# k^T v of two half batches in one TensorE block, with three t and kvz buffers

## The chip, the cores and the metric

The kernel runs on one core of a Trainium2 chip. The core has a matrix engine (TensorE, PE in the profile; the loads of its stationary operands are the row PEld), a vector engine (VectorE, DVE), a scalar engine (ScalarE, ACT), GpSimd (POOL) and a sync engine (SP). Each works through its own list of instructions in order, and semaphores hold an instruction back until what it needs is there. PE writes its results to PSUM, from which DVE and ACT read them. DMAs move data between device memory and SBUF; they are issued from the queues of SP and POOL. The metric is the time of one execution on the device, in microseconds (us); less is better.

## The reference

Inputs are q, k and v of 8 batches, 8 heads, 576 positions and a head size of 64, and the weights of 8 experts. First comes linear attention, then a layer of experts whose shares are balanced by eight rounds of row and column normalization.

```python
phi = lambda x: np.where(x > 0, x, np.exp(x) - 1.0) + 1.0
q_p, k_p = phi(q), phi(k)
kv = np.einsum('bhsd,bhse->bhde', k_p, v)
z = np.sum(k_p, axis=2)
num = np.einsum('bhsd,bhde->bhse', q_p, kv)
den = np.einsum('bhsd,bhd->bhs', q_p, z)[..., None] + 1e-06
x = (num / den)                      # transposed to 4608 tokens x 512
P = np.exp(x @ w_gate - max)
for _ in range(8):
    P /= P.sum(1, keepdims=True) + 1e-09
    P /= P.sum(0, keepdims=True) + 1e-09
    P *= N / E
for e in range(E):
    out += P[:, e:e + 1] * (np.maximum(x @ w1[e], 0.0) @ w2[e])
```

## The kernel before, in words

**Two parts.** The attention front produces x, transposed, in SBUF (`xT`: 128 partitions x 4 x 4608 tokens). Expert 0 is computed beside it, on the tokens that are ready, and experts 1 to 7 follow. Experts work on groups of 512 tokens: layer 1 (`hq`, L712 for the first two groups, L736 for the next, L858 for the later ones, which use a seven-product scheme for 2x2 blocks with sums prepared by DVE), then layer 2 (`ye`, L980 and L1098).

**The front** runs over 16 units (b, g): batch b and one half g of its eight heads, that is four heads. For each unit:

- k (576 KB, as f32), q and v (converted to 16 bits on the way) are loaded by DMAs issued on POOL (L386), a few of the first unit on SP. The k tiles have three buffers, q three, v three.
- ACT makes exp(k) (`ek`, L401), DVE makes max(k+1, 1) (`t`, L405) and the minimum of both (L409), which is phi(k). `t` has two buffers.
- PE forms k^T v and k^T 1 in one block (`f_kv`, L430): 18 matmuls with 64 rows each, two at a time on the upper and the lower half of the array, into a PSUM tile `kv_ps` that lies over two banks. The moving operand is the v tile, whose three planes are v, a plane of ones, and v of the other two heads. So the block is in another arrangement of the array than its neighbours, which use all 128 rows.
- Two copies (`f_z`, L337 on ACT or L339 on DVE) bring the result to SBUF as `kvz`, which has two buffers and zeros off its diagonal blocks, cleared once by DVE at the start.
- phi(q) is made likewise (L474, L477, L480), transposed by nine matmuls on PE (L485) into the two banks `att`, and copied to `qpT`.
- PE forms the denominators from `qpT` and `kvz` (`att`, L456); ACT takes Ln (L508) and Exp of the negative (L512), which is the reciprocal `rden`.
- PE forms the numerators (`num_ps`, L456), and DVE multiplies them by `rden` into `xT` (L527).

For the first two batches q, denominators and numerators are worked in two pieces, so that expert 0 can begin sooner; later ones in one or two equal halves. `kv_ps` and `num_ps` share one PSUM pool of one buffer (`p_kv`), so a numerator waits until the kvz copies are done, and a kv block until DVE has read the last numerator. After the third batch and after every odd batch PE forms the router's logits (L544).

**At the start** 40 matmuls on a tile of zeros (`yw <- warm`, L619) stand between the first instructions; their results aren't used. `warm` is 128 x 512. DVE clears the tiles and sets the three planes of ones (L631).

**The order.** Nothing is scheduled by hand in the code: `_Plan` records tasks with their engine, an estimate of their cost, what they depend on, the pools they take from and a priority, and `run` issues them in one order. For the front this order is written out, in the string `_FRONT`: each word is a task's number and its engine (p PE, a ACT, d DVE, g POOL, s SP, m a DMA in flight, n none). What comes after the front is ordered by the plan's estimates and priorities. A pool of n buffers makes a task wait for the users of the tile n places back.

**Gates.** For the last two units a tiny DMA on SP reads a corner of each loaded tile (L417), so that SP's stores behind it come after those loads; one POOL instruction (L421) does the same for POOL. Behind the gates SP stores x and its prepared sums to device memory (L759, L760, L791) for the experts 1 to 7. DVE makes these sums (L774 to L779) during and after the front.

**The end of the front.** When all of it is done its pools are closed, and two matmuls on zeros (L681) take the banks that expert 0 uses from then on.

Of the kernel before, what the change touches and what calls it, by code (L numbers as in the profile page):

```python
# [11 lines left out]
FP16 = mybir.dt.float16  # L12
# [5 lines left out]
class _Plan:  # L18
# [121 lines left out]
    1n 118n 123n 621n 44s 45m 0g 42s 43m 2p 48g 49m 3p 4p 46g 47m 5p 80g 81m 6p 7p 78g 79m 8p 57n 58a 59d 9p 82g 83m  # L140
    60d 10p 84g 85m 11p 12p 50a 51d 13p 14p 15p 16p 17p 18p 52d 19p 20p 53n 54p 63a 64d 21p 55d 22p 93n 61p 65d 128g
    129m 56a 23p 94a 62d 24p 25p 130g 131m 66p 26p 67d 86a 132g 133m 87d 68p 27p 134g 135m 28p 95d 69a 29p 88d 30p
    119g 120m 99a 71p 96d 89n 100d 90p 72a 101d 70a 164g 165m 97p 91d 102p 98d 31p 92a 166g 167m 32p 73a 103d 74p
    143n 170g 171m 104p 136a 75d 33p 34p 137d 121g 122m 76p 35p 105a 36p 77d 37p 144a 38p 107p 138d 106a 110p 168g
    169m 39p 108a 40p 111d 41p 139n 149a 145d 140p 146d 147p 141a 200g 201m 622p 148d 142a 150d 109a 124g 125m 151d
    112p 623a 152p 113d 202g 203m 624p 172a 179n 173d 204g 205m 632p 153a 174d 180a 154p 228g 229m 181d 175n 176p
    155a 182d 625d 633a 183p 177d 630p 184d 178a 156a 190p 631d 160p 232g 233m 191a 634p 161d 192a 230g 231m 157p
    635d 185a 196p 626p 258g 259m 186d 158a 187d 636p 126g 127m 197d 627a 207d 188p 637a 654n 661p 189d 159a 193p
    162p 260g 261m 628p 163d 638p 213n 206a 194a 208d 262g 263m 195a 629d 198p 640p 662a 199d 214a 114g 115m 209n
    655p 215d 216d 210p 656a 286g 287m 235d 217p 211a 657p 218d 288g 289m 663p 241n 234a 212a 236d 658d 219p 316g  # L150
    317m 237n 238p 220a 243d 664d 242a 221p 290g 291m 239d 659p 222a 244d 667p 660a 265d 223a 245p 240d 669p 116g
    117m 246d 224p 247p 225d 639p 271n 264a 248a 318g 319m 668d 226p 646a 641p 266d 272a 344g 345m 273d 249p 267n
    642p 227d 320g 321m 670a 274d 250a 268p 346g 347m 648d 275p 269a 270a 644p 299n 276d 251a 252p 277p 645p 253d
    278a 293d 292a 643p 301d 279p 687n 254p 294d 372g 373m 280a 665p 255d 300a 295n 256p 666d 322a 302d 296p 323d
    329n 257a 652a 688p 324d 400g 401m 297a 303p 298a 650d 348g 349m 281a 282p 690p 304d 376g 377m 330a 331d 675p
    357n 374g 375m 283d 691a 305p 351d 402g 403m 284p 306a 676p 285d 325n 350a 307p 332d 326p 683d 308a 430g 431m
    359d 673p 327a 689a 328d 309a 352d 333p 310p 334d 674p 378a 311d 335p 671p 379d 336a 312p 358a 337p 313d 353n
    672p 338a 360d 432g 433m 354p 339a 404g 405m 385n 361p 407d 486g 487m 355a 692p 413n 362d 356a 434g 435m 681a
    694p 387d 386a 693d 363p 380d 342p 364a 696p 460g 461m 343d 695a 314p 388d 406a 415d 340p 677p 315a 341d 381n
    414a 389p 697d 436a 495s 488g 489m 382p 390d 458g 459m 416d 365p 383a 698p 437d 366a 462g 463m 443n 384a 678p  # L160
    408d 367a 579d 391p 370p 392a 700p 371d 699a 393p 685d 496s 368p 394a 702p 369d 409n 701a 706p 438d 720n 395a
    580d 410p 586d 703a 445d 679a 417p 521g 522m 587d 411a 581d 707p 471n 412a 418d 517g 518m 444a 398p 419p 399d
    721p 420a 519g 520m 446d 472a 396p 421p 397d 439n 704p 422a 465d 440p 423a 473d 474d 447p 490g 491m 441a 722d
    705p 529g 442a 448d 464a 424p 723p 425d 534n 449p 466d 426p 450a 725p 427d 467n 714a 451p 726d 468p 452a 497s
    524d 526s 453a 475p 712d 527s 710p 528s 502n 476d 469a 582s 583m 470a 711p 724d 503a 493d 456p 477p 504d 708p
    478a 457d 535a 727p 588d 505d 589s 590m 479p 584s 585m 729p 536d 480a 537d 454p 481a 709p 591s 592m 455d 428p
    728d 492a 484p 716a 731p 485d 429a 730a 538p 494d 732a 482p 718a 539d 733p 498n 523a 483d 506p 499p 507a 525d
    600d 530n 735p 500a 501a 601d 741p 734d 761n 602d 508p 736d 603s 604m 531p 509a 605s 606m 593d 510p 532a 594d
    762p 511a 533d 595d 742p 757d 512a 596s 597m 598s 599m 515p 540p 749a 516d 764p 541a 758d 513p 765a 542p 514d
    737p 543a 759d 743p 544a 763d 547p 607d 766p 548d 744p 767a 760d 545p 608d 751a 768p 546d 770p 577n 769a 800d  # L170
    738p 609d 771a 801d 610s 611m 753d 549p 612s 613m 802d 754d 772p 550a 745a 803s 804m 551n 552d 774p 805s 806m
    773a 739p 775a 578p 755d 776p 858d 740p 756d 777a 614g 615n 618n 619g 620m 778d 808p 807n 553p 810p 809a 779d
    782p 811a 780d 822p 554d 783a 781d 816p 747a 812p 555d 788p 813a 823a 814p 786p 815a 828p 817d 556p 818p 829a
    557d 784p 789a 859d 819d 832p 785a 558d 820p 824p 792p 825a 821a 790p 860d 830p 833d 861s 862m 616g 617m 559p
    826p 1031s 1032m 793d 866p 827a 1088s 1089m 834p 560d 863s 864m 787d 867a 794p 835a 831d 870p 795a 865n 836d 880p
    871a 840p 837d 881a 561d 882p 841a 872p 883a 886p 846p 887a 884p 847a 838d 868p 873a 890p 791d 869a 850p 891d
    885a 842p 916d 917d 876p 843a 918d 892p 877d 874p 893a 888p 851d 878p 875d 852p 879a 839d 924p 889d 844p 925a
    974d 930p 894d 845a 938p 975d 853a 562p 848p 976d 931a 895d 977s 978m 928p 979s 980m 849d 923n 898p 929a 563d
    896d 939a 900p 919s 920m 899a 897d 921s 922m 944p 564d 926p 904p 927a 942p 905a 932p 901a 934p 933d 940p 908p
    935d 941a 1023d 945a 565p 936p 909d 948p 937a 902p 949d 943a 566d 982p 903a 567d 946p 983a 910p 906p 950p 981n  # L180
    947d 986p 951a 988p 911a 952d 568p 996p 987a 998p 953d 956p 997a 569d 999a 907d 984p 957a 570d 1004p 985a 962p
    989a 1002p 958p 1003a 963a 1000p 954d 959a 992p 1005d 1006p 955d 966p 1007d 964p 967d 571p 993d 960p 1024d 994p
    1025d 990p 995a 968p 1026d 1001a 991d 1008p 1033n 1034p 965d 1009a 1022n 1544n 1036p 572d 1035a 1012p 573d 1037a
    1040p 1042p 1041a 1038p 1044p 1039a 1013p 969a 1045d 574p 1043d 1010p 961d 1046p 1027d 1048p 1047a 575d 1050p
    1049a 576d 1011p 1051a 1054p 856d 1056p 1019d 1055a 1052p 651d 686a 1058p 1028d 1016p 1018a 1029d 713a 1091p
    1059d 1053a 1014p 653d 1057d 1015p 647d 1017p 854d 1020a 1092a 1093p 1021d 1090n 1547n 1060p 1094a 1030d 1097p
    1145s 1146m 1061a 1099p 1095p 1062d 1066p 1063d 1068p 1064d 1067a 1098a 1065d 1071p 649a 1101p 717a 1069d 1076p
    1070d 1096a 1102d 715a 1079p 1078d 1072a 1077d 970a 1103p 1073g 748d 1105p 750d 1107p 1548g 1549m 1100d 1106a
    1082p 1108a 682d 1104a 1111p 1084d 1113p 1081d 1112a 1109p 1080d 1074a 1115p 1083d 1110a 1075g 1148p 1114d 746a
    1150p 1116d 1085p 1149a 1151a 1117p 1087d 1147n 1154p 1086d 1118a 1202s 1203m 1156p 857a 1119d 1152p 1123p 1155a  # L190
    1120d 972d 1125p 1124a 1121d 915a 1128p 1122d 680a 1127d 1158p 1129a 684d 1133p 1153a 1126d 1130g 1159d 1136p
    1545g 1546m 1135d 1134d 1160p 1138d 1162p 1157d 1164p 1163a 1139p 752d 1165a 796d 1161a 1168p 1141d 1170p 1140d
    1169a 1166p 1131a 1172p 1167a 1205p 1173d 1207p 1206a 1137d 1142p 1208a 1174p 1143d 1204n 1211p 1171d 1175a 1259s
    1260m 1213p 913a 1144d 1209p 1176d 1180p 1212a 1177d 1182p 1181a 1178d 719a 1185p 1179d 798a 1183d 1215p 1188a
    1184d 1190p 1210a 1216d 1186a 1214d 1193p 914a 1187g 971d 1217p 1191d 1132g 1219p 1192d 1221p 1189g 1220a 1196p
    1222a 1218a 1225p 1198d 1227p 1194d 1226a 1223p 1197d 1229p 797d 1224a 1262p 1228d 1264p 1263a 1230d 1199p 1265a
    1195d 1231p 1200d 1261n 1268p 1201d 1232a 1316s 1317m 1270p 973a 1233d 1266p 1237p 1269a 1234d 1239p 1235d 1238a
# [23 lines left out]
def kernel(  # L221
# [10 lines left out]
    nc = tc.nc  # L232
# [127 lines left out]
    def att(b, g):  # L360
# [73 lines left out]
        def f_za(_):  # L434
            gz["tile"] = kvz_t[(len(p_kvz["order"]) - 1) % 2]
# [821 lines left out]
```

## Time and profile before

| what | us |
| --- | --- |
| median of three runs | 958.1 (957.68 to 958.19) |
| profiled execution, its own time | 958.06 |
| span of the profiled execution | 955.9 |
| PE busy | 947.0 |
| DVE busy | 784.1 |
| ACT busy | 583.5 |

The span runs from the first to the last instruction that the profile shows. The tables name an engine, a line of the kernel, the tile that is written and those read, how often, the busy time and the mean duration. Matmuls are pipelined: one of 512 columns is shown as 379 ns long, while the next begins 216 ns after it. So the starts of instructions tell more of PE than its busy time does.

### The profile page before, as it was taken

How to read it: one execution, taken by the hardware profiler on the slowest of the kernel's cores; microseconds unless marked ns; L12 is line 12 of the kernel's file. 1: busy time of each engine (PE TensorE's matmuls, PEld its weight loads, DVE VectorE, ACT ScalarE, POOL GpSimd, SP SyncE). 2: the span in 40 equal slices, each digit the busy share in tenths (PEclk: the TensorE clock that was granted, in tenths of full speed). 3: DMA queues.
4: the chain of work that ended last, by engine and by line, in shares of the span. 5: the costliest groups of instructions: out<-in, count | busy, mean ns of one | idle time of the engine just before them, and what ended most of it. 6: DMA issues, size and time to landing. Idle time of an engine off the chain costs nothing.

```text
span 955.9 us, 21249 instructions
## 1 busy us (share of the span) xinstructions
PE 947.0 (99%) x8634; PEld 810.4 (85%) x8634; DVE 784.1 (82%) x1508; ACT 583.5 (61%) x1047; POOL 146.8 (15%) x211
## 2 busy tenths in 40 slices
PE   8999999999999999999999999999999999999998
PEld 4765588788888888888888888888888888888886
DVE  7899999998888888878887888878887888877775
ACT  7999766576555555555555555555555555555552
POOL 7432000011102111211112111110112111111110
PEclk9999999999999999999999999999999999999999
DMA  9998492172127222542227222362226222235554
GB/s 239 265 230 179 167 251 79 39 159 68 66 75 162 76 79 78 131 113 79 79 77 167 79 78 78 95 149 77 79 78 132 95 69 73 72 99 166 166 166 110
DMA packets 47101, 112.81 MB, mean 118 GB/s; under 512 B 4444, under 2 KB 27484, under 8 KB 47004
## 3 DMA queue, kind: packets, MB, share of 16 engines
q1 hardware_dynamic: 21340, 75.84, 24.1%
q0 software_dynamic: 25264, 35.11, 19.5%
q8 instruction: 67, 1.10, 0.5%
q10 hardware_dynamic: 400, 0.52, 0.2%
q14 instruction: 30, 0.25, 0.1%
HBM read 119.69 MB, written 17.69 MB: 144 GB/s over the span
## 4 chain that ended last, share of the span: by engine, by line
PE 95%; DVE 2%; DMA 1%; ACT 1%; POOL 0%; issue 0%; SPq 0%; DVEq 0%; ACTq 0%
PE ye L1098 36%; PE hq L858 24%; PE R L858 12%; PE Zye L858 6%; PE Zye L1098 6%; PE ye L980 4%; PE hq L736 2%; PE hq L712 1%; DMA w<-in_moe_w_dram 1%; PE kv_ps L430 1%; PE att L456 1%; PE num_ps L456 1%; PE att L485 1%; DMA kin<-in_k_dram 0%; DVE xT L527 0%
## 5 line engine op out<-in xcount | busy, mean ns | idle before, releaser
L1129 DVE SCALAR_TENSOR_TENSOR acc<-ye,P_sb,acc 128x256 f32<-128x256 f32 x620 | 267.7, 479 | 123.2 <-PE ye L1098 121.8
L858 PEld LDWEIGHTS <-W 128*128 128x128 f16 x2144 | 209.8, 98 | 24.9
L1098 PEld LDWEIGHTS <-S 128*128 128x128 f16 x1984 | 194.1, 98 | 22.5
L1139 POOL TENSOR_TENSOR acc<-acc,st 128x256 f32<-128x256 f32 x124 | 88.5, 733 | 686.5 <-ACT st L1136 686.5
L1098 PE MATMUL ye<-T,S 128*128 128x256 f16 x1488 | 192.8, 273 | 0.0
L858 PEld LDWEIGHTS <-w 128*128 128x128 f16 x1608 | 157.3, 98 | 19.6 <-issue 0.5
L1098 PEld LDWEIGHTS <-h 128*128 128x128 f16 x1584 | 155.0, 98 | 18.1 <-issue 0.2
L893 ACT ACTIVATE h<-hq 128x512 f16<-128x512 f32 x134 | 80.1, 598 | 141.9 <-PE hq L858 139.2
L858 PE MATMUL R<-xs,W 128*128 128x256 f16 x1008 | 151.2, 273 | 0.0
L858 PE MATMUL hq<-xs,W 128*128 128x256 f16 x1008 | 151.2, 273 | 0.0
L858 PE MATMUL hq<-xs,w 128*128 128x256 f16 x1008 | 140.9, 273 | 0.3 <-DVE h L896 0.3
L890 ACT ACTIVATE h<-Zye 128x512 f16<-128x512 f32 x134 | 80.1, 598 | 40.0 <-PE Zye L858 40.0
L1136 ACT ACTIVATE st<-Zye,P_sb 128x256 f32<-128x256 f32 x124 | 52.6, 471 | 71.1 <-PE Zye L1098 70.9
L873 ACT COPY Zye<-hq 128x512 f32<-128x512 f32 x134 | 77.7, 580 | 27.9 <-PE hq L858 27.7
L880 ACT COPY s<-hq 128x512 f32<-128x512 f32 x126 | 73.5, 583 | 34.6 <-PE hq L858 34.0
L1069 DVE TENSOR_TENSOR S<-h 128x1024 f16<-128x1024 f16 x124 | 85.4, 688 | 11.2 <-ACT h L893 11.1
L896 DVE CUSTOM_DVE_ANT_0 h<-R,s 128x512 f16<-128x512 f32 x126 | 86.6, 687 | 9.4 <-ACT s L880 9.4
L896 DVE CUSTOM_DVE_ANT_0 h<-hq,s 128x512 f16<-128x512 f32 x126 | 86.6, 687 | 3.5 <-PE hq L858 3.4
L858 PE MATMUL Zye<-xs,w 128*128 128x256 f16 x504 | 75.6, 273 | 0.0
L887 ACT COPY s<-R 128x512 f32<-128x512 f32 x126 | 74.5, 591 | 0.1
L1098 PE MATMUL ye<-w,h 128*128 128x256 f16 x528 | 68.4, 273 | 0.0
L1098 PE MATMUL Zye<-w,h 128*128 128x256 f16 x528 | 68.4, 273 | 0.0
(124 smaller groups left out, 988.7 us busy)
## 6 DMA issues: line engine op xcount, KB each, us to landing
xs<-xd SPq DMA_DIRECT2D x63, 896.0 KB, 4.8
kin<-in_k_dram POOLq DMA_DIRECT2D x15, 576.0 KB, 7.1
out_dram<-acc SPq DMA_DIRECT2D x67, 128.0 KB, 2.4
w<-in_moe_w_dram POOLq DMA_DIRECT2D x16, 512.0 KB, 8.8
w<-in_moe_w_dram POOLq DMA_DIRECT2D x7, 1024.0 KB, 13.0
vv<-in_v_dram POOLq DMA_DIRECT2D x16, 288.0 KB, 7.4
qin<-in_q_dram POOLq DMA_DIRECT2D x12, 288.0 KB, 7.8
xd<-acc SPq DMA_DIRECT2D x5, 512.0 KB, 3.4
```

The lines of the kernel that those rows point to most:

```text
L858: nc.tensor.matmul(dst[:, p, :], lhsT=lhs(p, c), rhs=rhs(c), start=(first and p == 0 and c == 0), stop=(c == 1), skip_group_check=True)
L873: nc.scalar.copy(out=Zt[1], in_=gX["tile"])
L880: nc.scalar.copy(out=gs2["tile"], in_=gX["tile"])
L887: nc.scalar.copy(out=gs5["tile"], in_=gR["tile"])
L890: nc.scalar.activation(out=hd(0, 0), in_=Zt[1], func=AF.Relu)
L893: nc.scalar.activation(out=hd(1, 0), in_=gX["tile"], func=AF.Relu)
L896: nc.vector._custom_dve(TENSOR_ADD_SAT, out=dst, in0=ps, in1=sb, s0=3.0e38, s1=0.0)
L1069: nc.vector.tensor_tensor(out=Sx[:, i], in0=a0, in1=a1, op=op)
L1098: nc.tensor.matmul(bank(g_)[:, s, :], lhsT=lhs(s, kk), rhs=rhs(kk), start=(new and s == 0 and kk == 0), stop=(kk == 3), skip_group_check=True)
L1129: nc.vector.scalar_tensor_tensor(out=dst(), in0=bank(g_)[:, s, :], scalar=P_sb[:, gg, e:e + 1], in1=dst(), op0=ALU.mult, op1=ALU.add)
L1136: nc.scalar.mul(out=gst["tile"], in_=bank(g_)[:, s, :], mul=P_sb[:, gg, e:e + 1])
L1139: nc.gpsimd.tensor_tensor(out=dst(), in0=dst(), in1=gst["tile"], op=ALU.add)
```

## The change

- From the third batch on (`MB = 2`) the kv blocks of both units of a batch become one block of 36 matmuls (`att_kv`), into the same PSUM tile: the first unit's result in columns 0 to 191 of both banks, the second's in 192 to 383. Four copies, one after another, bring it to two `kvz` tiles. `att` is split into `att_k` (loads and phi(k)), `att_kv` and `att_q` (all from phi(q) on); the first unit of a batch is held until the second's k is there.
- `t` and `kvz` have three buffers, not two. The third kvz is cleared by ACT, which multiplies `warm` by zero.
- The v tiles become rows of one tile with a shared plane of ones, seven planes in place of nine. `warm` shrinks to 128 x 128, read four times over through a broadcast.
- The SP gates are for v alone: two of them, and the one on POOL; the four for k and q go.
- The first seed copy of each unit of seven products also depends on the two matmuls on zeros that close the front.
- `_FRONT` is another order, for the tasks as they now are. Numbers of tasks shift, so nearly all of its words differ. In the built programs PE's instructions are the same in number and shape. kvz copies within the front: 25 on ACT and 7 on DVE before, 16 and 16 after.

```diff
 _FRONT = """
...
 """
...
-    HB = 2
+    GN = ("v",)
+    HB, MB, NZ, NT = 2, 2, 3, 3
...
-    vv_t = [fp.tile([P, 3, NJ, D], FP16, tag=f"vv{i}", name=f"vv{i}", bufs=1) for i in range(NV)]
-    kvz_t = [fp.tile([P, 2, 2, P], FP16, tag=f"kvz{i}", name=f"kvz{i}", bufs=1) for i in range(2)]
+    vv = fp.tile([P, 2 * NV + 1, NJ, D], FP16, tag="vv", name="vv", bufs=1)
+    vv_t = [vv[:, NV - 1 - i:NV + 2 + i:i + 1] for i in range(NV)]
+    kvz_t = [fp.tile([P, 2, 2, P], FP16, tag=f"kvz{i}", name=f"kvz{i}", bufs=1) for i in range(NZ)]
...
-    p_t, p_tq, p_kvz, p_qpT, p_rden = (S_.pool(2) for _ in range(5))
+    p_t, p_kvz = S_.pool(NT), S_.pool(NZ)
+    p_tq, p_qpT, p_rden = (S_.pool(2) for _ in range(3))
...
-        for nm in ("k", "q", "v") if n >= 14 else ():
+        for nm in GN if n >= 14 else ():
...
+    def att_kv(ks):
+        gkv, gzs = S_.grp(p_kv), [S_.grp(p_kvz) for _ in ks]
+        pr = ks[-1][1]
 
         def f_kv(_):
             gkv["tile"] = kvps.tile([P, 2, 512], FP32, tag="kv", name="kv_ps")
-            for j in range(NJ):
-                for hh in range(2):
-                    s = slice(64 * hh, 64 * hh + 64)
-                    nc.tensor.matmul(gkv["tile"][:, hh, 0:3 * D].rearrange("p (r d) -> p r d", r=3),
...
+            for i, k_ in enumerate(ks):
+                gin, gt = k_[4], k_[7]
+                for j in range(NJ):
+                    for hh in range(2):
+                        s = slice(64 * hh, 64 * hh + 64)
+                        nc.tensor.matmul(gkv["tile"][:, hh, 3 * D * i:3 * D * i + 3 * D].rearrange("p (r d) -> p r d", r=3),
+                                         lhsT=gt["tile"][s, j, :, :].rearrange("p r d -> p (r d)"), rhs=gin["v"]["tile"][s, :, j, :],
+                                         start=(j == 0), stop=(j == NJ - 1))
...
+        tkv = fadd(("pe", 0.02 + 0.83 * len(ks)), f_kv, deps=[x for k_ in ks for x in (k_[8], k_[5]["v"])] + tza, acq=[gkv],
+                   use=[x for k_ in ks for x in (k_[4]["v"], k_[7])], prio=pr, cfg=1)
+        out_, zp = [], []
+        for i, gz in enumerate(gzs):
+            kv_id.append(tkv)
+            tz = []
+            for r in range(2):
+                def f_z(e, r=r, gz=gz, o=3 * D * i + 64 * r):
+                    s = slice(64 * r, 64 * r + 64)
+                    src = gkv["tile"][s, :, o:o + 2 * D].rearrange("p h (z d) -> p h z d", z=2)
+                    dst = gz["tile"][s, :, :, 64 * r:64 * r + 64]
+                    copy(e, dst, src if r == 0 else src[:, :, ::-1])
+                tz.append(fadd({"dve": 0.43, "act": 0.37}, f_z, deps=[tkv, *zp], use=[gkv, gz], prio=pr))
+                zp = tz[-1:]
+            out_.append((gz, tz))
+        return out_
...
+    def att(b, g):
+        k_ = att_k(b, g)
+        if b < MB:
+            att_q(b, g, k_, att_kv([k_])[0])
+        elif g == 0:
+            held.append(k_)
+        else:
+            ks = [held.pop(), k_]
+            zs = att_kv(ks)
+            for h_ in range(2):
+                att_q(b, h_, ks[h_], zs[h_])
...
-    warm = const.tile([P, 512], FP16, tag="warm", name="warm")
+    warm = const.tile([P, P], FP16, tag="warm", name="warm")
+    warm_w = warm.unsqueeze(1).to_broadcast([P, 4, P])
...
-        nc.tensor.matmul(yw[0], lhsT=warm[:, 0:P], rhs=warm, start=True, stop=True)
+        nc.tensor.matmul(yw[0].rearrange("p (a b) -> p a b", a=4), lhsT=warm, rhs=warm_w, start=True, stop=True)
...
-    for t in vv_t:
-        nc.vector.memset(t[:, 1], 1.0)
-    for t in kvz_t:
-        nc.vector.memset(t, 0.0)
+    nc.vector.memset(vv[:, NV], 1.0)
+    for i, t in enumerate(kvz_t):
+        if i < 2:
+            nc.vector.memset(t, 0.0)
+        else:
+            nc.scalar.mul(out=t.rearrange("p a b c -> p (a b) c"), in_=warm_w, mul=0.0)
...
-        c1 = add(("act", 0.58), f_seed, deps=[m1], acq=[gZ], use=[gX], prio=ui - 400.0)
+        c1 = add(("act", 0.58), f_seed, deps=[m1, t_zt], acq=[gZ], use=[gX], prio=ui - 400.0)
```

More of the change, by code (lines that the diff above doesn't have):

```diff
@@ L145 @@
[L145 to L154, printed above, removed]
@@ L358, in att_bank, with att_k @@
         return at2[:, (len(p_att["order"]) - 1) % 2]
-    def att(b, g):
+    def att_k(b, g):
         n = 2 * b + g
@@ L422, in att @@
             gates[n] = add(("pool", 0.15), f_gate, deps=[tin["v"]], use=[gin["v"]], prio=pr)
-        gkv, gz = S_.grp(p_kv), S_.grp(p_kvz)
+        return n, pr, qj, cs, gin, tin, tinq, gt, tk
+    def att_kv(ks):
+        gkv, gzs = S_.grp(p_kv), [S_.grp(p_kvz) for _ in ks]
+        pr = ks[-1][1]
         def f_kv(_):
             gkv["tile"] = kvps.tile([P, 2, 512], FP32, tag="kv", name="kv_ps")
-            for j in range(NJ):
-                for hh in range(2):
-                    s = slice(64 * hh, 64 * hh + 64)
-                    nc.tensor.matmul(gkv["tile"][:, hh, 0:3 * D].rearrange("p (r d) -> p r d", r=3),
-                                     lhsT=gt["tile"][s, j, :, :].rearrange("p r d -> p (r d)"), rhs=gin["v"]["tile"][s, :, j, :],
-                                     start=(j == 0), stop=(j == NJ - 1))
@@ L434, in f_za @@
-        def f_za(_):
-            gz["tile"] = kvz_t[(len(p_kvz["order"]) - 1) % 2]
-        tza = fadd(("none", 0.0), f_za, deps=[tk, tin["v"]], acq=[gz], prio=pr)
-        tkv = fadd(("pe", 0.85), f_kv, deps=[tk, tin["v"], tza], acq=[gkv], use=[gin["v"], gt], prio=pr, cfg=1)
-        kv_id.append(tkv)
-        tz = []
-        for r in range(2):
-            def f_z(e, r=r):
-                s = slice(64 * r, 64 * r + 64)
-                src = gkv["tile"][s, :, 64 * r:64 * r + 2 * D].rearrange("p h (z d) -> p h z d", z=2)
-                dst = gz["tile"][s, :, :, 64 * r:64 * r + 64]
-                copy(e, dst, src if r == 0 else src[:, :, ::-1])
-            tz.append(fadd({"dve": 0.43, "act": 0.37}, f_z, deps=[tkv, *tz], use=[gkv, gz], prio=pr))
+            for i, k_ in enumerate(ks):
[6 more added lines that the diff above has]
+                                         start=(j == 0), stop=(j == NJ - 1))
@@ new lines, in att_kv, with f_za @@
+        tza = []
+        for gz in gzs:
+            def f_za(_, gz=gz):
+                gz["tile"] = kvz_t[(len(p_kvz["order"]) - 1) % NZ]
+            tza.append(fadd(("none", 0.0), f_za, deps=[x for k_ in ks for x in (k_[8], k_[5]["v"])] + tza, acq=[gz], prio=pr))
+        tkv = fadd(("pe", 0.02 + 0.83 * len(ks)), f_kv, deps=[x for k_ in ks for x in (k_[8], k_[5]["v"])] + tza, acq=[gkv],
+                   use=[x for k_ in ks for x in (k_[4]["v"], k_[7])], prio=pr, cfg=1)
+        out_, zp = [], []
@@ L680, in f_zt @@
         for i in range(2):
-            nc.tensor.matmul(Zt[i].rearrange("p a b -> p (a b)"), lhsT=warm[:, 0:P], rhs=warm, start=True, stop=True)
+            nc.tensor.matmul(Zt[i].rearrange("p a (c b) -> p (a c) b", c=2), lhsT=warm, rhs=warm_w, start=True, stop=True)
     t_close = add(("none", 0.0), f_close, deps=front_ids, prio=0.0)
```

146 lines of the change are left out of this document (78 added, 68 removed).

## The prediction

> **What bounds the kernel now.** I read the page first, then stages, then the instructions of TensorE (PE) in order of time, and last the waits.
>
> ```profile
> span 955.9 us, 21249 instructions
> PE 947.0 (99%) x8634; PEld 810.4 (85%) x8634; DVE 784.1 (82%) x1508; ACT 583.5 (61%) x1047; POOL 146.8 (15%) x211
> PEclk9999999999999999999999999999999999999999
> ...
> PE 95%; DVE 2%; DMA 1%; ACT 1%; POOL 0%; issue 0%; SPq 0%; DVEq 0%; ACTq 0%
> ```
>
> PE is the bound at a full granted clock. The attention front shares PE with expert 0, so the end moves only with PE's work or with the time in which PE stands still. Four stages:
>
> ```profile
> 0.00:20.80 20.80, 16.77 (x131) 8.84 (x132) 15.34 (x34) 14.42 (x21) 14.73 (x25) 1.00 1.06 244
> 20.80:34.98 14.18, 13.98 (x130) 11.00 (x131) 11.92 (x23) 13.11 (x22) 7.95 (x12) 1.00 1.20 249
> 34.98:120.54 85.56, 85.17 (x829) 52.68 (x828) 79.98 (x139) 77.33 (x111) 20.52 (x31) 1.00 0.85 206
> 120.54:260.00 139.46, 139.46 (x1239) 120.76 (x1238) 124.00 (x254) 90.51 (x168) 12.17 (x16) 1.00 0.42 109
> ```
>
> The columns are PE, PE's weight loads, DVE, ACT, POOL, clock, DMA share, GB/s. Busy time hides short stalls, so I use starts in the timeline:
>
> ```profile
> 46.52 1.03 PE L980 MATMUL ye<-w,h 128*128 128x512 f16 x4
> 47.48 0.92 PE L430 MATMUL kv_ps<-vv,t 64*128 64x192 f16 x18
> 48.33 0.68 PE L485 MATMUL att<-ident,tq 128*128 128x128 f16 x9
> 48.84 1.03 PE L980 MATMUL ye<-w,h 128*128 128x512 f16 x4
> 49.71 0.41 PE L456 MATMUL num_ps<-qpT,kvz 128*128 128x288 f16 x2
> ```
>
> Four 512-column matmuls take 0.87 us (48.84 to 49.71), 0.216 each; by other such pairs a 256-column one takes 0.109, a 288-column one 0.122, a transpose 0.056, a logit one 0.025. Ahead of the kv block the same four take 0.96: 0.095 us goes on entering it. The block takes 0.85; nine pairs, each at 192 columns (0.084, the two run at once), are 0.756, so leaving it costs 0.095. One kv block on its own costs 0.19 us beside its work.
>
> From 34.98 to 120.54 (the end of the front) the matmuls, each at its own pitch, sum to 81.46 us; 85.56 went by. PE stood still 4.10 us: 12 kv blocks at 0.19 are 2.26, and 1.84 are waits. ACT is as full as PE there (29.17 of 30 us from 60 to 90). Up to 34.98 us PE did 27.18 us of work (8.6 of it the 40 dummy matmuls): 7.8 us lost, to loads and latency. From 120.54 to 260 it loses 0.7.
>
> ```profile
> PE hq L712 <- DMA w<-in_moe_w_dram: 0.4, 1, 0.4
> ```
>
> That wait, from those of the first 27 us, says that expert 0 starts (20.80) when half of w1 lands.
>
> **The change part by part** (PE's instructions are the same in number and shape: 8,626 matmuls each, 40 of them dummies).
>
> *Merged blocks.* Twelve blocks become six of 36 matmuls, so six entries and exits go: 6 x 0.19 = -1.1 us, all on PE's path. Bounds: -1.3 (the 0.21 that rounded starts give) to 0, if PE only waits longer for ACT.
>
> *What a merged block adds.* It waits for two t and two v, and its PSUM tile (one buffer, shared with num) is held for four kvz copies in place of two.
>
> ```profile
> L337 ACT CAST kvz<-kv_ps x20: 350/367/378, 36.9 to 106.8; 64x256 f16<-64x256 f32 x20
> L339 DVE CAST kvz<-kv_ps x4: 406/427/428, 40.6 to 107.3; 64x256 f16<-64x256 f32 x4
> ```
>
> In the built program the four run one behind the other, across both engines: about 0.37+0.37+0.43+0.43 plus a handoff, 1.7 us. Until the next num, PE has 2.5 to 4.0 us of other work in the new order (transposes, four to eight expert matmuls): hidden when both engines are free. An ACT instruction of 1.16 us in the way (ek, eq) gives 2.8 against 2.5. Between 0 and 1.2 us over six blocks; I take +0.3, nearer the free case, since only three of the six have the short cover of 2.5. Behind a waiting num stand the expert matmuls and then the xT product on DVE.
> [...]
>
> *Third t and kvz buffers.* t for the next batch can be made while a block waits; price 0, or a gain counted under the order. The third kvz is cleared by ACT (a half-microsecond instruction by its nearest row, the 128x512 copy, 0.58) in the 1.66 us that ACT idles before the first load lands; if that load came 1 us sooner, up to 0.4 would show. The v tiles share one plane of ones: two memsets of 0.538 us go from DVE, which waits for the first load anyway: 0.
>
> *Dummy operand read four times over.* No row has it; the nearest, the kv matmul with its operand in three pieces, streams at the same 0.42 ns a column as a plain one. 0; the dummies fill waits, so +1 at worst.
>
> *Loads.* In the new queue order k of (0,1) goes ahead of v of (0,0), which lands near 9.5 in place of 7.7 us; dummies and transposes cover that. v of (0,1) comes 1.4 us sooner. Half of w1 goes ahead of v and the rest of q of (1,0) and lands near 18, not 20.66. The other half has the same loads ahead as before: near 26.5. The first half of w2 now has the second k of batch 2 ahead (1.4 us): 32.7, not 31.3; PE wants it near 33.5, so a slip beyond 0.8 us shows. From batch 3 on a v load waits on POOL for a whole block, with q and k loads queued behind; the next block is 11.3 us of PE work away and a v load takes 7.4 (median to landing), so 4 us are spare and k has a batch more.
>
> *Gates.* Four tiny SP DMAs go; the store behind them waits for DVE's sums, so 0. DVE's block of x_blocks in the front shrinks by three instructions of 0.42 (moved later, where DVE has room): 0.
>
> *New order, first 35 us.* I carried the durations of the rows through the new order by hand, along PE, ACT and DVE. The first expert matmul comes near 19.0 with 12.85 us of PE work before it (before: 20.80, 13.83): 0.8 ahead. Then kv of (1,0) and the transposes and num of (1,1) wait some 0.3 each for ACT's reciprocals and DVE's copies, and at w1's second half 0.25 is left. At the first wait on expert 0's second group (27.78 us of work) PE stands near 35.3: 0.3 ahead. Take -0.3, with -1.0 and +1.0 as ends (one ACT instruction more or less in each wait).
>
> *New order, 35 to 120 us.* Summing the durations ahead of each result that PE waits for, and PE's work up to the wait: in the order of before the least distance to ACT falls from +1.1 (PE work 40 to 50) to -0.8 (70 to 80), where ACT is late. In the new one it stays between +1.7 and +2.7. Nine kvz copies (3.3 us) leave ACT for DVE, three expert copies (1.8) come back. Against that, ACT's own waits for PE have -1.8 to -2.5 in the new order (before -1.3 to +0.6), so the loop PE-ACT has no more room than it had. Between 0 and -1.8; I take -1.1, three fifths, since a level distance does not pile up.
>
> *After the front.* The planner's order changes, the work doesn't; PE stalls 0.7 there before. 0, +-0.3.
>
> Sum: -1.1 +0.3 -0.3 -1.1 = -2.2 us. The profiled execution took 958.06 us (span 955.9 and 2.2 around it), the median of the runs is 958.1: 955.8.
>
> **The rivals.**
> *The waits stay (same, 956.2 to 959.9).* ACT is 97% busy from 60 to 90 us and the loop PE-ACT is as tight; then only the entries and exits go, or not even those. -1.1 alone gives 956.9. For it: ACT's row; against it: ACT idles 8.2 us of the stage, 2.6 waiting for PE's att.
> *The hold decides (slower).* Place: the num behind a merged block. Each copy waits behind one instruction on its engine: four copies and two waits of 1.16 give 3.9 us against 2.5 to 4.0, and the DVE copies also stop DVE, which is 93% busy, so the delay comes back at xT. At +0.9 a block, 5.4 in all, less 2.5 of gains: 961.0. It decides from +0.6 a block. For it: in the trace the two copies of single blocks end 0.8 to 2.9 us after the block; against it: the copies stand side by side in the new order on most blocks.
> *The start slips.* If k of (0,0) and w1 land as late as before, the first stage loses 1: 957.1, inside the first rival.
>
> **How the numbers follow.** Forecast (faster) 0.55, waits stay 0.27, hold or another new wait 0.18. 0.2% (1.9 us) is about what a measurement of this kernel can tell from no change: faster is below 956.2, slower above 960.0. Lowest sum -1.3 -1.0 -1.8 +0 = 954.0, of which I allow 954.2. The forecast's own range is 954.2 to 956.9. Half of the slower case lies above 960.0, so 954.2 to 960.0 leaves out about 0.1 on top and 0.1 below.
>
> **What would show it.** Merged blocks of about 1.6 us from start to next matmul with one entry of 0.095; first expert matmul near 19; from 35 us to the dummies that close the front about 2.5 us of stall, not 4.1; ACT idle less. Wrong would be: num or att waiting over 0.3 us for kvz copies after merged blocks; expert matmuls waiting for ACT or DVE copies at 35 to 110; a load landing after PE wants it; a stall after 120 us that was not there.

## The result, and the profile after

The changed kernel takes 956.9 us, median of 22 runs (955.62 to 958.09), against 958.08 of the kernel before, median of 22 on the same chip: a ratio of 0.9987, with a 95% interval of 0.9981 to 0.9993. A second comparison gave 957.43 against 958.29, again 0.9987 (0.9978 to 0.9996). So 1.2 us are gained (0.7 to 1.8 by the first interval): a gain, and one that stays within the 0.2% that was called no change.

The page of the changed kernel, its first part, its granted clock, and the shares of the chain:

```profile
span 954.5 us, 21233 instructions
PE 946.7 (99%) x8634; PEld 811.1 (85%) x8634; DVE 781.3 (82%) x1506; ACT 583.1 (61%) x1048; POOL 147.6 (15%) x211
PEclk9999999999999999999999999999999999999999
...
PE 93%; DVE 4%; issue 1%; ACT 1%; DMA 1%; POOL 0%; DVEq 0%; POOLq 0%; ACTq 0%
```

PE still bounds the kernel at full clock. The same four stages, cut at the first expert matmul (19.76 us; before 20.80), with the columns as before:

```profile
0.00:19.76 19.76, 17.15 (x109) 8.27 (x109) 12.08 (x27) 13.98 (x21) 14.54 (x25) 1.00 1.05 248
19.76:35.00 15.24, 14.98 (x156) 12.26 (x155) 13.53 (x27) 14.21 (x24) 7.78 (x11) 1.00 1.21 244
35.00:120.50 85.50, 84.63 (x830) 53.08 (x829) 80.87 (x145) 74.60 (x108) 21.47 (x30) 1.00 0.85 198
120.50:260.00 139.50, 139.50 (x1248) 121.53 (x1247) 122.13 (x250) 93.09 (x175) 13.70 (x19) 1.00 0.43 114
```

In the third row DVE has 0.9 us more to do than before and ACT 2.7 us less. A merged block in PE's timeline:

```profile
61.67 1.66 PE L435 MATMUL kv_ps<-vv,t 64*128 64x192 f16 x36
63.48 0.68 PE L501 MATMUL att<-ident,tq 128*128 128x128 f16 x9 [0.15 <-DVE tq L496]
63.99 1.03 PE L1012 MATMUL ye<-w,h 128*128 128x512 f16 x4
```

The 36 matmuls run through without a step between the halves. Behind the block stands a new wait: the transposes are held up by DVE's product `tq`.

To add up the losses I use one measure for all kernels: PE's *standstill*, which is the start of a matmul in the trace less the work of all matmuls ahead of it, each at its own pitch (a k^T v block without its entry and exit). Each row is one profiled execution, with its time:

| kernel | to 35 us | 35 to 121 | 121 to 245 | that execution |
| --- | --- | --- | --- | --- |
| before | 7.8 | 4.1 | 0.70 | 958.06 |
| changed | 7.9 | 3.2 | 0.21 | 956.36 |
| changed, a second time | 7.7 | 4.9 | 0.22 | 957.78 |

From 245 us on both lose the same within 0.1 us. The gain of the first profile is 0.9 us in the stage of the merged blocks and 0.5 behind the front. In the second profile the stage gained nothing, though kernel and order are the same, and the whole execution was 1.4 us longer; the median of the changed kernel, 956.9, lies between the two. A single profile of this stage is good to about 1.5 us; the experiments have to be read with that.

### The profile page after: what moved, and what is told of

It reads as the page before. It is cut to its first block, busy times and chain, and to the rows that moved or that the text cites. A ratio compares the mean times of both kernels' runs of the same rounds, so it can differ in the third digit from the quotient of the medians.

```text
span 954.5 us, 21233 instructions
## 1 busy us (share of the span) xinstructions
PE 946.7 (99%) x8634; PEld 811.1 (85%) x8634; DVE 781.3 (82%) x1506; ACT 583.1 (61%) x1048; POOL 147.6 (15%) x211
## 4 chain that ended last, share of the span: by engine, by line
PE 93%; DVE 4%; issue 1%; ACT 1%; DMA 1%; POOL 0%; DVEq 0%; POOLq 0%; ACTq 0%
PE ye L1130 36%; PE hq L890 25%; PE R L890 12%; PE Zye L890 6%; PE Zye L1130 6%; PE ye L1012 3%; DVE xT L543 1%; PE yw L649 1%; PE hq L768 1%; DMA qin<-in_q_dram 1%; PE hq L744 1%; PE kv_ps L435 1%; DVE t L408 1%; DVE t L404 1%; PE num_ps L472 0%
```

## The experiments

All ratios are to the kernel before, run beside it on the same chip.

**Breaks put back into the merged blocks.** A break is one exit from the 64-row matmuls and one entry back. One tiny matmul over all 128 rows between the two halves makes one, and undoes the merging and nothing else:

```diff
             for i, k_ in enumerate(ks):
+                if i == 1:
+                    nc.tensor.matmul(gkv["tile"][:, 0, 504:512], lhsT=warm, rhs=warm[:, 0:8], start=True, stop=True)
```

The second kernel puts three of them there with two of 64 rows between, so three breaks per block; the third has the same five tiny matmuls, but the three of 128 rows ahead of the block, so no break.

> The changed kernel with one tiny matmul of 128 rows (8 columns) put between the two halves of each of the six double k^T v blocks: each half is entered and left by itself again, as before the change, and nothing else differs. Theory 'the switches are the gain': TensorE has no slack here, six exits and entries at 0.19 us and six tiny matmuls at 0.03 to 0.06 us come back in full, +1.3 to +1.5 us against the changed kernel, the time of the kernel before or a little more (958.2 to 958.4). Rival 'VectorE paces the stage': behind three of the six blocks TensorE waits 0.22 to 0.26 us for VectorE's tq, and these waits swallow the longer block: +0.6 to +0.8 us (957.5 to 957.7). Rival 'order and buffers are the gain': +0.2 us or less.

> The same place, with three tiny matmuls of 128 rows and two of 64 rows between them in each of the six double blocks: 18 more exits and entries and 30 tiny matmuls. 'The switches are the gain': 18 x 0.19 = 3.4 us on top of what the 30 tiny matmuls cost by themselves (next run), 960.5 to 961.8. 'VectorE paces the stage': the first 0.25 us behind three of the blocks are swallowed, the rest counts, 2.6 us on top of the next run. 'Order and buffers': under 0.5 us on top of it.

> The control for the run before: the same 30 tiny matmuls, but the three of 128 rows ahead of each double block and the two of 64 rows inside it, so that no exit or entry is added. All theories: 30 x 0.03 to 0.06 us, +0.9 to +1.8 us against the changed kernel at most, and no exit or entry step more in the trace.

Measured: one break 957.90 us, ratio 0.9997 (0.9988 to 1.0005); three breaks 959.81, 1.0016 (1.0007 to 1.0024); none 957.23, 0.9992 (0.9983 to 1.0001). Three breaks in PE's timeline:

```profile
62.82 0.92 PE L441 MATMUL kv_ps<-vv,t 64*128 64x192 f16 x18
63.67 0.18 PE L432 MATMUL kv_ps<-warm 128*128 128x8 f16 x1
63.78 0.18 PE L433 MATMUL kv_ps<-warm 64*128 64x8 f16 x1
...
64.22 0.92 PE L441 MATMUL kv_ps<-vv,t 64*128 64x192 f16 x18
65.07 0.68 PE L507 MATMUL att<-ident,tq 128*128 128x128 f16 x9
```

Each change between 64 and 128 rows puts 0.11 us between matmuls of 8 columns, which follow each other every 0.026 us when nothing changes (12 such pairs in the third kernel take 0.306). Over the 18 breaks the steps sum to 4.37 us; less the tiny matmuls (0.026 each) and the ordinary step behind the last pair of a half (0.08), 3.1 us are left, 0.17 a break. The one break of the first kernel lengthens a block from 1.59 to 1.81 us, 0.19 beside its tiny matmul. This is about the price that the prediction read from the row, 0.19.

The time shows less than the price. Kernels two and three have the same instructions and differ by 18 breaks: 2.58 us between the medians (2.3 +- 1.2 by the intervals), 0.14 a break where the steps say 0.17. The interval doesn't exclude the full price, but the timeline shows where some of it goes: with the breaks, the transposes behind the block start at once. In the kernel with one break the waits for `tq` behind three of the blocks, 0.219, 0.236 and 0.261 us in the changed kernel, are 0, 0.015 and 0.044 with the exit taken off. So the theory that the switches are the gain stands, with a discount: part of what PE saves in a merged block it waits off right behind it, because `tq` isn't done. How large the discount is stays open. By the price of 0.14 six breaks are worth about 0.9 us. But a block takes off its wait once, however many breaks it has: with one break in each of six blocks, 0.66 of the 1.31 us that breaks and tiny matmuls add stand where waits stood, so that in that trace six breaks alone are worth 0.5 us. Its time is 1.0 us above the changed kernel's by the two ratios, known to about 1 us, and can't tell this from the full price. The rival that order and buffers alone bring the gain is out, by the second and third kernel.

**The nine copies back to ACT.** In the written order, nine words:

```diff
-222d 223d 279d 280d 281d 337d 338d 390d 391d
+222a 223a 279a 280a 281a 337a 338a 390a 391a
```

> The changed kernel with nine of its thirteen kvz copies of the stage on VectorE moved back to ScalarE, in their places in the order (20 on ScalarE and 4 on VectorE, as before the change). 'VectorE, loaded by the new order, is what makes the waits left in the front': the waits of TensorE for VectorE's xT and tq at 63.5, 67.5, 81.1 and 88.3 us (0.90 us together) fall to 0.3 us or less, VectorE's 80.9 us in the stage fall by 9 x 0.43 = 3.8 and ScalarE's 74.6 rise by 3.3, and the kernel is 0.3 to 0.8 us faster, 956.1 to 956.6. Rival 'the work is only shifted': ScalarE gets late in VectorE's place, waits for its kvz and rden come for those that go, within 0.3 us of the changed kernel either way. Rival 'the written order fits only these engines': +0.5 us or more.

Measured: 959.87 us, 1.0017 (1.0008 to 1.0026), 2.9 us slower than the changed kernel by the two ratios. The standstill from 35 to 121 us is 7.2 us. PE's waits from 50 to 95 us (us in all, times, longest):

```profile
PE num_ps L472 <- ACT kvz L336: 1.3, 2, 0.8
PE att L472 <- ACT qpT L336: 0.6, 1, 0.6
PE att L472 <- ACT rden L524: 0.4, 1, 0.4
```

The second rival: ACT, although it has more room in the stage than DVE, can't take the copies in those places, since Exp and Ln of 0.74 to 1.17 us stand ahead of them. The move of nine copies to DVE belongs to this order. Whether DVE's load keeps the waits that are left, this run can't say: the three waits for `tq` behind the blocks are still there (0.22, 0.24 and 0.29 us), and ACT's have come beside them.

**Less work for DVE.** First the sums over x of the first five token groups on GpSimd, in the changed kernel and in the one before:

```diff
-                tt_ = nc.vector.tensor_tensor
+                tt_ = (nc.gpsimd if early else nc.vector).tensor_tensor
```

> The changed kernel with the sums over x of the first five token groups (15 steps, 20 VectorE instructions of 0.42 us, 8.4 us, nearly all of them between 77 and 120 us) on GpSimd, in the same places of the order; every other queue is as it was. 'VectorE paces the stage of the changed kernel': TensorE's waits behind VectorE from 81 to 112 us (81.14, 88.25, 93.47, 101.50, 111.47: 1.17 us together, and part of 0.16 at 90.89) fall to 0.4 us or less, those before 77 us (0.80 us) stay, and the kernel is 0.6 to 1.0 us faster, ratio to the kernel before 0.9977 to 0.9981. Rival 'the waits are a matter of the written order': the waits stay within 0.3 us, ratio 0.9984 to 0.9990. Rival 'GpSimd holds VectorE up': VectorE's instructions beside the sums get longer, or the loads that GpSimd issues come later, and the waits grow: ratio 0.999 or more.

> The same move in the kernel before: its 15 steps of sums over x on GpSimd, same places. If VectorE paces only the changed kernel (before: ScalarE 77.3 and VectorE 79.9 us of 85.5 busy, waits for both), the gain is smaller than in the changed kernel: 0 to 0.5 us, since of the waits between 77 and 120 us only about 0.24 are for VectorE (83.32, and 88.27 and 78.44 are for ScalarE). If VectorE paces both, 0.6 us or more. If GpSimd holds VectorE up, slower in both.

Measured: 964.17 us, 1.0067 (1.0054 to 1.0079), and 968.63, 1.0106 (1.0091 to 1.0121). GpSimd holds VectorE up, far more than I had allowed. DVE's groups from 77 to 121 us, in the changed kernel and then with the sums on GpSimd (busy, mean ns of one), with one of GpSimd's:

```profile
L496 DVE TENSOR_TENSOR tq<-tq,eq 128x1152 f16<-128x1152 f16 x5 | 3.8, 750 | 0.0
L493 DVE TENSOR_SCALAR tq<-qin 128x1152 f16<-128x1152 f16 x5 | 2.3, 451 | 0.0
L807 DVE TENSOR_TENSOR acc<-xT 128x512 f16<-128x512 f16 x5 | 2.1, 418 | 0.0
```

```profile
L496 DVE TENSOR_TENSOR tq<-tq,eq 128x1152 f16<-128x1152 f16 x5 | 8.2, 1635 | 0.2
L493 DVE TENSOR_SCALAR tq<-qin 128x1152 f16<-128x1152 f16 x5 | 3.6, 713 | 0.0
L543 DVE TENSOR_TENSOR xT<-num_ps,rden 128x576 f16<-128x576 f32 x13 | 9.8, 752 | 3.0 <-PE num_ps L472 2.5 <-ACT rden L528 0.5
L807 POOL TENSOR_TENSOR acc<-xT 128x512 f16<-128x512 f16 x5 | 6.5, 1304 | 0.0
```

The product `tq`, with both operands in SBUF, takes over twice as long, 1.64 us in place of 0.75; the one with an operand in PSUM (L543) is as it was, 752 ns against 754. In the kernel before `tq` goes from 0.75 to 1.31 us. Why they take longer, no trace shows. Since the move lengthens VectorE's own work, these two runs say nothing of what DVE's load is worth. For that, the sums were cut instead: 32 of every 256 tokens are computed, seven eighths are left out, and x is stored in place of the sums.

```diff
-                lo, hi = xT[:, :, t0:t0 + 256], xT[:, :, t0 + 256:t0 + 512]
+                w = 32 if early else 256
+                T = T[:, :, :, 0:w]
+                lo, hi = xT[:, :, t0:t0 + w], xT[:, :, t0 + 256:t0 + 256 + w]
```

> The changed kernel with the 20 sums over x of the first five token groups computed for 32 of each 256 tokens only (left out: the other seven eighths; what is stored in their place are x itself, so that the transfers stay). VectorE loses 20 x 0.3 = 6 us of work between 77 and 121 us, and no engine gets anything more. 'VectorE paces TensorE there': of the waits at 81.14, 88.25, 93.47, 101.50 and 111.47 (1.17 us) 0.8 us or more go, and with them 0.7 to 1.1 us of the time, ratio to before 0.9976 to 0.9980. Rival 'three engines are full at once' (60 to 105 us: VectorE 95 to 100 %, ScalarE 84 to 98 %, TensorE 96 to 100 % busy): ScalarE's chain ends last in place of VectorE's and 0.5 us or less is won, 0.9982 or more.

> The same left out of the kernel before. Its waits between 77 and 121 us that name VectorE are 0.10 (83.32) and, behind ScalarE's, 0.26, 0.09 and 0.09. 'VectorE paces the changed kernel more than the one before': 0 to 0.4 us faster than before, less than the cut brings in the changed kernel. If the cut brings the same in both, the shift of nine copies from ScalarE to VectorE is not what keeps the waits of the changed kernel.

Measured: 961.56 us, 1.0032 (1.0021 to 1.0044), and 957.68, 0.9994 (0.9986 to 1.0003). The first figure is mostly an effect of the cut itself: a store now reads x and holds back the step that overwrites it.

```profile
137.08 0.69 DVE L1106 TENSOR_TENSOR xT<-h 128x1024 f16<-128x1024 f16 x1 [3.41 <-DMA xd<-xT]
```

This stops PE for 3.4 us, until 140.5, behind the stage in question. Ahead of it the two profiles can be read: from 77 to 121 us DVE has 38.4 us of work in place of 41.4 (3.0 less, not the 6 I had expected), and PE's standstill there is 1.7 us in place of 1.9; in the kernel before it is 1.6 with and without. The sum of the changed kernel hides two effects. The five waits behind DVE that the expectation names are 1.17 us together; in the second profile each is the same within 0.01 us. With the sums cut they are 0.39. One of them, in the changed kernel and then with the sums cut:

```profile
92.87 0.41 PE L472 MATMUL att<-qpT,kvz 128*128 128x288 f16 x2
93.47 0.41 PE L472 MATMUL num_ps<-qpT,kvz 128*128 128x288 f16 x2 [0.19 <-DVE xT L543]
```

```profile
93.75 0.41 PE L472 MATMUL att<-qpT,kvz 128*128 128x288 f16 x2
94.11 0.41 PE L472 MATMUL num_ps<-qpT,kvz 128*128 128x288 f16 x2
```

The two denominators take 0.245 us, so PE waits 0.36 us for `xT` in the first and 0.12 in the second. Against this, the profile of the cut kernel has waits of 0.48 and 0.22 us at 91.3 and 91.8, where the first profile has 0.16: a q load came late, as below. So in the trace the theory holds for these waits: three microseconds less for DVE take 0.8 us of them away in the changed kernel and nothing in the one before. In the time it isn't shown.

**Two copies in place of four.** The three kvz buffers become one tile, and each copy takes both halves.

```diff
+    kvz = fp.tile([P, NZ, 2, 2, P], FP16, tag="kvz", name="kvz", bufs=1)
+    kvz_t = [kvz[:, i] for i in range(NZ)]
...
+                    dst = (kvz[s, i0:i0 + 2] if i0 < NZ - 1 else kvz[s, ::-(NZ - 1)])[:, :, :, :, 64 * r:64 * r + 64]
+                    src = src if r == 0 else src[:, :, :, ::-1]
+                copy(e, dst, src)
```

> The changed kernel with its three kvz buffers in one tile, and the four copies behind each double block (64 x 256 each, 0.37 us on ScalarE, 0.43 on VectorE) made two (64 x 512, both halves at once, at 0.60 and 0.69 us as other copies of 512 columns): seven on VectorE and five on ScalarE in place of thirteen and eleven, in the places of the first two. The hold of the PSUM tile shrinks from 1.6 to 1.3 us, VectorE loses 0.7 us of work and ScalarE 1.1, while the first half's den and num can start only when both halves are copied (0.25 to 0.5 us later), and the second half's earlier. 'The copies and the two engines' load hold TensorE up': 0.3 to 0.8 us faster than the changed kernel, ratio to before 0.9978 to 0.9984. 'The first half's start decides': 0.3 to 1.0 us slower than the changed kernel, 0.999 or more.

Measured: 957.29 us, 0.9992 (0.9983 to 1.0001): no faster than the changed kernel, perhaps a little slower. Its copies in the stage (min/median/max ns):

```profile
L339 DVE CAST kvz<-kv_ps x7: 675/694/695, 41.3 to 103.2; 64x512 f16<-64x512 f32 x7
L337 ACT CAST kvz<-kv_ps x5: 565/578/581, 40.7 to 89.7; 64x512 f16<-64x512 f32 x5
```

Of these copies there are 12 in place of 24, and VectorE's takes 0.69 us where two of 0.43 were. PE still loses 4.3 us in the stage, which is within what two profiles of the changed kernel differ by. The run changes two things at once, a shorter hold and a later start of the first half, so it doesn't price the hold alone. The waits do: in the changed kernel only one of 0.16 us, at 90.9, ends with a kvz copy. The hold of the PSUM tile by four copies, a rival in the prediction, isn't what PE waits for here.

**The orders behind the front, exchanged.** Each kernel keeps its own written order as far as the last attention step; from there (the tail) it takes the order of the other. As a measure the changed kernel ran once more.

```diff
-_FRONT of one kernel, all words
+_FRONT of one kernel up to its last attention step, then the other's words that are left
```

> The kernel before with its own written order as far as its last attention step (VectorE's last xT), and from there the written order of the changed kernel (the same steps with other numbers). Nothing of the merged blocks is in it. Theory 'the 0.5 us after the front come from the new order of the steps behind it': the five waits of TensorE at 144.6, 145.2, 161.7, 198.9 and 219.0 us (0.51 us together) are gone, 0.4 to 0.6 us faster than before, ratio 0.9994 to 0.9996. Rival 'they hang on where the front leaves the engines': the waits or others of the same size come back, within 0.2 us of before. Rival 'the order fits only its own front': slower by 0.5 us or more.

> The other half of the exchange: the changed kernel with its merged blocks and its own written order as far as its last attention step, and from there the written order of the kernel before. 'The steps behind the front, newly ordered, are worth 0.5 us': the waits of TensorE for VectorE's h and acc near 144, 145, 199 and 219 us come back, TensorE's waits between 121 and 245 us rise from 0.2 to 0.7 us, and the kernel is 0.4 to 0.6 us slower than the changed one run beside it, ratio to the kernel before 0.9992 to 0.9994. Rival 'they hang on where the front leaves the engines': within 0.2 us of the changed kernel, no such waits. Rival 'an order fits only its own front': 1 us slower or more.

> The changed kernel unaltered, beside the run before it on the same chip, as its measure. All theories: the ratio to the kernel before of the first comparison, 0.9981 to 0.9993, and waits of TensorE in the stage from 35 to 121 us within 0.3 us of those of its first profile (1.41 us beside the k^T v blocks); if they differ by more, waits of that size are chance from one execution to the next, and differences of the other runs below 0.5 us say nothing.

Measured: before with the tail of the changed kernel 957.95 us, 0.9999 (0.9991 to 1.0008); changed with the tail of before 957.38, 0.9993 (0.9984 to 1.0002); the changed kernel again 957.43, 0.9987 (0.9978 to 0.9996). The traces are clear where the times are not. From 121 to 245 us PE stands still for 0.21 to 0.23 us in every kernel with the new tail (eight profiles, leaving out the one with the store in the way and those with the sums on GpSimd) and 0.46 to 0.70 in every one with the old tail (three profiles). So the waits belong to the order of the tail, whichever front is ahead of it, and make 0.2 to 0.5 us of standstill. The times don't show it: by the ratios it is 0.6 us in one direction, within the intervals (the medians, 957.38 and 957.43, show nothing), and nothing in the other. In the profile of the kernel before with the new tail PE's last matmul comes 0.9 us sooner than before, yet the span is as long: its last two stores land 3.5 us after their issue, not 2.6. Why, and whether this is so in each of its executions, stays open.

The second profile of the changed kernel differs from the first by more than 0.3 us, 1.6 us beside the k^T v blocks. By what I had written, single differences below that say little. Some 0.6 us of it are two waits for DVE, 0.31 us for `xT` at 36.7 and 0.28 for `tq` at 38.1, which the first profile doesn't have and whose cause stays open. The rest, 1.0 us, can be followed:

```profile
88.25 0.68 PE L501 MATMUL att<-ident,tq 128*128 128x128 f16 x9 [0.17 <-DVE tq L496]
88.76 1.03 PE L1012 MATMUL ye<-w,h 128*128 128x512 f16 x4
89.62 1.03 PE L768 MATMUL hq<-xT,w 128*128 128x512 f16 x4
90.48 0.41 PE L472 MATMUL att<-qpT,kvz 128*128 128x288 f16 x2
```

```profile
88.66 0.68 PE L501 MATMUL att<-ident,tq 128*128 128x128 f16 x9 [0.17 <-DVE tq L496]
89.17 1.03 PE L1012 MATMUL ye<-w,h 128*128 128x512 f16 x4
90.36 1.02 PE L768 MATMUL hq<-xT,w 128*128 128x512 f16 x4 [0.16 <-ACT h L773]
91.86 0.40 PE L472 MATMUL att<-qpT,kvz 128*128 128x288 f16 x2 [0.48 <-DVE qpT L338]
```

The first fence is the first profile, the second the second. The stretch from the transposes to the denominators is 2.23 us in the one and 3.20 in the other. Ahead of it ACT's exp(q) waits for a load, in the first profile and in the second:

```profile
87.22 1.16 ACT L490 ACTIVATE eq<-qin 128x1152 f16<-128x1152 f16 x1 [0.49 <-DMA qin<-in_q_dram]
```

```profile
88.66 1.16 ACT L490 ACTIVATE eq<-qin 128x1152 f16<-128x1152 f16 x1 [1.52 <-DMA qin<-in_q_dram]
```

ACT's relu and the kvz copy, in line behind that exp, come later by the same 1.03 us, and PE's waits for them by 1.0. Of the nine profiles of kernels with the new front whose loads are untouched, counting these two, seven have this wait, from 0.44 to 1.52 us; the two without it are those with five tiny matmuls per block. None of the three with the old front has it. The traces point to GpSimd's queue; the load is the first of the two q loads here:

```profile
77.00 0.73 POOL L385 DMA_DIRECT2D kin<-in_k_dram  x1 [2.78 <-ACT h L773]
77.72 1.50 POOL L385 DMA_DIRECT2D vv<-in_v_dram  x2
79.22 1.43 POOL L385 DMA_DIRECT2D qin<-in_q_dram  x2
```

```profile
74.08 0.72 POOL L386 DMA_DIRECT2D qin<-in_q_dram  x1 [2.63 <-ACT eq L474]
74.79 0.73 POOL L386 DMA_DIRECT2D kin<-in_k_dram  x1
75.52 0.77 POOL L386 DMA_DIRECT2D vv<-in_v_dram  x1
81.97 0.72 POOL L386 DMA_DIRECT2D vv<-in_v_dram  x1 [5.69 <-DVE tq L477]
```

First the changed kernel, then the one before. In the changed kernel q stands behind a k load that waits for its buffer until 77.00 us, and behind two v loads. Five loads, 1.7 MB, leave within 3.7 us, and the q load goes out at 79.22 and lands about 8.0 us later, at the edge of need; in the second profile it takes 9.0. Over the nine profiles it takes 7.6 to 9.1. Before, three loads go out together there (four near 67 us), and the q load of that time takes 5.8. That the order of the loads makes this wait is read from the traces; a kernel with the q load moved ahead was not tried.

## Why the prediction was right, and where it was not

The time lies at the upper end of the forecast's own range, 1.1 us above the forecast. But the case that came is not the likeliest one: it is the rival "the waits stay", whose own figure for "only the entries and exits go" was 956.9. That the median meets it to the digit is luck: the entries and exits bring less than 1.1, and a term put at 0 brings the rest. Step by step:

- **Six entries and exits, -1.1.** The price is about right: 0.19 by the row, 0.17 to 0.19 by the breaks. Their net worth is less, 0.5 to 0.9 us by the two ways of counting above, since `tq` is waited for behind three blocks. (The pages show 8,634 matmuls in both kernels, not 8,626; that they are the same in number holds.)
- **The hold of four copies, +0.3.** Hardly seen: one num wait of 0.16 us at 90.9 us. The rival that lets the hold decide is out for this order. It isn't idle, though: with nine copies back on ACT, two num waits for kvz copies make 1.3 us, as the rival has it for an Exp in the way. The four copies run in line: behind the block at 61.67 us ACT's two take from 63.84 to 64.59 and DVE's two from 65.05 to 65.90, and the program makes each depend on the one before it. No run let two go at a time.
- **The waits from 35 to 120 us, -1.1.** This step failed, by the most: 1.84 us became 2.06 in the first profile, and 3.7 in the second. The argument was a level distance to ACT. That distance did its work, for the waits named after ACT fell from 0.64 to 0.2 us; but the prediction gives no such distance for DVE, which was 93% busy before and was given nine copies more. Waits of 0.72 us for `tq` and about 1 us for `xT`, both DVE's, took their place; with 3 us less for DVE from 77 us on, 0.8 of the 1.17 us there are gone. Those behind the late q load come on top. The waits, from 35 to 121 us, as the view of waits lists them for the second profile; for the first it lists the first and the third of them:

```profile
PE att L501 <- DVE tq L496: 0.5, 3, 0.2
PE att L472 <- DVE qpT L338: 0.5, 1, 0.5
PE num_ps L472 <- DVE xT L543: 0.2, 1, 0.2
PE hq L768 <- ACT h L773: 0.2, 1, 0.2
```

The view leaves out the short waits and counts the stretch in which PE is idle; the sums above are of steps between matmuls.

- **The loads.** The prediction had q and k loads in line behind a v load that waits on GpSimd, and found 4 us to spare. It worked that out for v alone. In the trace a k load and two v loads hold up the q load, which has nothing to spare: 0.5 us late in the first profile, at little cost to PE, and a microsecond later in the second, paid in full. In part the failed step above fails by this one.
- **The start, -0.3.** The first expert matmul came at 19.76 us, later than the 19.0 worked out, and at 35 us PE had stood still 0.1 us longer than before. Profiles of the new front up to there run from 7.4 to 8.1 us (of the old front 7.4 to 8.4), so a gain of 0.3 can be neither shown nor excluded.
- **After the front, 0.** It was -0.5 in the first profiles, and in the traces of the exchange 0.2 to 0.5. The prediction gave the order there to the planner and put the term at nothing. But the written order goes on long past the front: the waits that the exchange moved lie as late as 219 us.
- **Third buffers, gates, dummies, memsets, 0.** Nothing in the traces speaks against it; none of them was run alone.

In the first profiles' terms: -1.1 of switches, +0.2 of waits in place of -1.1 and +0.3, +0.1 at the start and -0.5 behind the front make -1.3, against the 1.4 us between the two spans and the 1.2 between the medians. (The forecast's own terms give 955.9 from 958.06, where it says 955.8.)

## What to carry to other kernels

A saving on the engine that bounds a stage is worth its price less what the next result makes that engine wait: look at the instruction behind the saved piece and at who makes its operand. When a new order is judged by how far each engine is ahead, count this for the engine that is given more work too, put the load queue in the list of engines, and follow every load that stands behind one that waits for its buffer, not only the one that waits. And take a second profile of the same kernel before explaining a microsecond from one: here the two differ by 1.6.

## What the runs showed of the hardware that was not expected

- Elementwise work on GpSimd is dear here twice over: 1.3 us for a sum that VectorE makes in 0.42, and VectorE's `tq` products beside it grow from 0.75 to 1.64 us on average. By the ratios the move costs 7.7 us in the changed kernel and 10.2 in the one before, a part of it with PE at a lower clock: in the changed kernel it is granted at 0.65 from 105.0 to 108.7 us, behind 5.0 us in which PE was busy for 3.02.
- After a stop of 3.4 us, from 137.1 to 140.5, PE came back slower. In the kernel with the sums cut, in windows ahead of the stop, of its end, and after (columns as in the stages, PEclk third from last):

```profile
130.00:136.00 6.00, 6.00 (x58) 5.40 (x56) 3.08 (x8) 4.22 (x8) 0.00 (x0) 1.00 1.17 272
140.50:145.40 4.90, 4.90 (x30) 3.71 (x31) 4.69 (x12) 2.63 (x5) 0.00 (x0) 0.65 0.22 89
145.40:150.00 4.60, 4.60 (x46) 4.14 (x44) 2.95 (x6) 2.08 (x5) 0.00 (x0) 1.00 0.00 2
```

The granted clock is 0.65 over 4.9 us. PE goes on at 140.5 us, at its full pitch at first, and from 142.0 to 145.2 fifteen matmuls of 256 columns follow each other every 0.214 us in place of 0.109, about half as fast, which makes 1.6 us more. That the stop is what slowed PE is my reading of the order of the two; how long a stop it takes, no run shows.
